# A GELU layer forward and backward: the first 256 rows of x turned by products on TensorE instead of by the DMA, the first q behind four units' pieces, and one transposed weight load in two

## The chip, the cores and the metric

One core of one Trainium2 chip runs the whole kernel in one launch. The metric is the device time of an execution in microseconds (us), the median of several. Engines are named as the profile names them: PE is TensorE (matmul; PEld is its weight load), DVE is VectorE, ACT is ScalarE, POOL is GpSimd, and SP is SyncE, which here only issues DMAs.

## The reference, cut to what matters

```python
B, S, D, F = 1, 2048, 448, 1792          # everything bf16
def forward(x, w1, b1, w2, b2):
    h = gelu(einsum("bsd,df->bsf", x, w1) + b1)      # tanh form of gelu
    return einsum("bsf,fd->bsd", h, w2) + b2
out, vjp = jax.vjp(forward, x, w1, b1, w2, b2)
return (out, *vjp(grad_out))             # out, gx, gw1, gb1, gw2, gb2
```

So three products come first for every block of rows: u = x·w1 (before the gelu), out = h·w2, and q = grad_out·w2ᵀ. Then gh = q·gelu'(u), and gx = gh·w1ᵀ. At the end come gw1 = xᵀ·gh and gw2 = hᵀ·grad_out, and the two bias sums.

## The kernel before, in words

**Stages.** The 2048 rows are four blocks of 512, taken in the order of `ROW0` (L54), so block 0 is rows 512 to 1023. F = 1792 is seven pairs of 128-column tiles, taken in the order `FP` = 1, 2, 3, 4, 5, 6, 0 (L56), so the first pair is columns 256 to 511. A step is one pair of one block, 28 in all. Both operands of u and q lie transposed in SBUF: `xT` and `gT` hold a block as 128 partitions by four slices of D (the fourth only half real, since 448 = 3·128 + 64), `w2T` holds w2 in the same way. All three come in by DMAs that transpose on the way, issued by SP in program order (L99 to L186). After the 28 steps (to about 177 us) come gw1 and gw2.

**What a step does.** PE makes u of the pair in two PSUM banks (three products of full depth 128 per tile, and one of depth 64, "the tail"). ACT copies u out with the bias (`copy_u`, L339; for the first two pairs DVE copies one of the two tiles), squares it (L354), makes gelu (L351, which writes `hT`) and a tanh (L363). DVE makes the slope of the gelu from these and at last multiplies it with q from PSUM (`dve_gh`, L401, which frees q's banks). Output units (`Unit`, L420: 128 rows of out or gx, in one bank) collect pieces, two products for each pair, as their `hT` or `ghT` comes.

**Products of half height.** Most products are issued as two of 64 rows each, one on the lower and one on the upper half of the array, side by side (`side_by_side`, L308; all have line 265, in `half_product`). A pair of them takes the array as long as one product of full height. Where one bank gets a product from the other half than before, `half_product` puts in a wait on the earlier one (L260 to L264). Products of full height are `pe_u_fulls` (L238, line 244), the tails with zeros (L502, line 505) and a unit's `emit` (L428, line 431).

**The start.** The order is written out by hand under `manual_schedule`. SP issues the transposing load of `xT[0]` in two halves of 256 rows (L146, L149), then a part of w1 (L154), w2 (L155), all of `gT[0]` (L156), `w2T` for columns 256 to 511 (L157), and so on. ACT issues w1 and its last 64 rows (`load_rest`) for columns 256 to 511 (L147, L148); behind its table load and a small activation (L151) it issues w1 for 512 to 767 (L152) and `load_rest` for 512 to 1023 (L153). POOL issues b1, which DVE turns into a column per tile (L192, L193) for `copy_u`. PE begins with `NWAKE` = 11 products on constant ones (L190), whose result nobody reads. Then it makes u of pairs 0, 1 and 2 (L507, L513, L519; pair 0 over the two halves of `xT[0]`), opens four units (L520 to L523), and L524 to L549 order what follows: pieces of units 0 and 1 for pair 0 at full height, pieces of units 2 and 3 side by side, the tails of u 2 and q 0, the rest of q 0 with units 2 and 3 between, and so on. The loop at L556 does the steps from 1.

Of the kernel before, what the change touches and what calls it, by code (L numbers as in the profile page):

```python
# [10 lines left out]
ALU = mybir.AluOpType  # L11
BF16 = mybir.dt.bfloat16
F32 = mybir.dt.float32
# [6 lines left out]
def kernel(  # L20
# [15 lines left out]
    nc = tc.nc  # L36
    P = 128
    B, S, D = x.shape
# [4 lines left out]
    KF = D // P  # L43
    DL = D - KF * P
    SB = 512
# [3 lines left out]
    NSTEP = NB * NPAIR  # L49
    NSINGLE = 12  # L50
    LEAD = 2
    NWAKE = 11
    STG = 5
    ROW0 = [SB, 2 * SB, 3 * SB, 0]  # L54
    WIDE = (0, 1)
# [3 lines left out]
    x2 = x.rearrange("b s d -> (b s) d")  # L59
# [4 lines left out]
    const = ctx.enter_context(tc.tile_pool(name="const", bufs=1))  # L64
# [14 lines left out]
    w2T = const.tile([P, KF + 1, F], BF16, name="w2T")  # L79
# [8 lines left out]
    def one_bank(n, name):  # L88
        return psum.tile([P, SB], F32, name=name, tag=f"one{n}")

    def two_banks(n, name):
        return psum.tile([P, 2, SB], F32, name=name, tag=f"two{n}")

    xT, gT = {}, {}

    def wide(src, r0, n, shift):
        return bass.AP(src.tensor, src.offset + r0 * D - shift, [[D, n], [1, (KF + 1) * P]])
# [11 lines left out]
    def load_g(b):  # L109
        t = blk.tile([P, KF + 1, SB], BF16, name="gT", tag="gT")  # L110
        r0 = ROW0[b]
        if b in WIDE:
            nc.sync.dma_start_transpose(out=t[:], in_=wide(g2, r0, SB, DL))
        else:
            nc.sync.dma_start_transpose(out=t[:, 1:KF + 1, :], in_=g2[r0:r0 + SB, DL:D])
            nc.sync.dma_start_transpose(out=t[:, 0, :], in_=g2[r0:r0 + SB, 0:P])
        gT[b] = t

    def load_w1(eng, f0, f1):
        return eng.dma_start(out=w1_f[:, :, f0:f1], in_=w1[0:KF * P, f0:f1].rearrange("(kt p) f -> p kt f", p=P))  # L120

    def load_rest(eng, f0, f1):
        return eng.dma_start(out=wt1[0:DL, f0:f1], in_=w1[KF * P:D, f0:f1])

    def behind(eng, transfer):
        tc.add_manual_dep(eng.nop().ins, transfer.ins.name, mybir.DependencyInfo(mybir.DependencyClass.Sync, mybir.DependencyReason.DATA),
                          reason="loads behind what is needed first")

    def load_w2(eng, t0, t1):
        return eng.dma_start(out=w2_sb[:, t0:t1, :], in_=w2[t0 * P:t1 * P, :].rearrange("(ft p) d -> p ft d", p=P))  # L130

    def load_w2T(f0, f1):
        if f0 > 0:
            nc.sync.dma_start_transpose(out=w2T[:, :, f0:f1], in_=wide(w2, f0, f1 - f0, DL))
        else:
            nc.sync.dma_start_transpose(out=w2T[:, :, 16:f1], in_=wide(w2, 16, f1 - 16, DL))
            nc.sync.dma_start_transpose(out=w2T[:, 1:KF + 1, 0:16], in_=w2[0:16, DL:D])

    AZ = tmp.tile([P, 12, SB], BF16, name="AZ", tag="AZ", bufs=1)
    ones = nc.const_aps.tensor(1.0, [P, SB], BF16)  # L140
    nc.vector.memset(wt1[DL:P, 256:768], 0.0)
    nc.gpsimd.memset(b1_rows[:], 0.0)
    nc.gpsimd.dma_start(out=b1_rows[0:NF, :], in_=b1.rearrange("(ft p) -> ft p", p=P))
    xT[0] = blk.tile([P, KF + 1, SB], BF16, name="xT", tag="xT")
    halves = [slice(0, SB // 2), slice(SB // 2, SB)]
    nc.sync.dma_start_transpose(out=xT[0][:, :, halves[0]], in_=wide(x2, ROW0[0], SB // 2, 0))  # L146
    load_w1(nc.scalar, 256, 512)  # L147
    load_rest(nc.scalar, 256, 512)  # L148
    nc.sync.dma_start_transpose(out=xT[0][:, :, halves[1]], in_=wide(x2, ROW0[0] + SB // 2, SB // 2, 0))  # L149
    warm = stg.tile([P, 1], F32, name="warm", tag="warm", bufs=1)  # L150
    behind(nc.scalar, nc.scalar.activation(out=warm[:], in_=ones[:, 0:1], func=ACT.Gelu_apprx_tanh))  # L151
    load_w1(nc.scalar, 512, 768)  # L152
    load_rest(nc.scalar, 512, 1024)  # L153
    load_w1(nc.sync, 768, 1024)  # L154
    load_w2(nc.sync, 2, 4)  # L155
    load_g(0)  # L156
    load_w2T(256, 512)  # L157
    load_w2(nc.sync, 4, 6)
    load_w1(nc.sync, 1024, 1280)
    load_rest(nc.sync, 1024, F)  # L160
# [27 lines left out]
    pw = two_banks(1, "pw")  # L188
    for w in range(NWAKE):
        nc.tensor.matmul(pw[:, 0, :], lhsT=ones[:, 0:P], rhs=ones, start=True, stop=True)  # L190
    for c in range(P // 32):
        nc.vector.transpose(b1_t16[c * 32:(c + 1) * 32, :], b1_rows[:, c * 32:(c + 1) * 32])  # L192
    nc.vector.tensor_copy(out=b1T[:], in_=b1_t16[:, 0:NF])  # L193
# [2 lines left out]
    PU, PQ = {}, {}  # L196
# [4 lines left out]
    def cols(p, a):  # L201
        return slice((2 * FP[p] + a) * P, (2 * FP[p] + a + 1) * P)
# [28 lines left out]
    def open_u(f):  # L231
        b, p = divmod(f, NPAIR)
        if p == 0:
            hT[b] = blk.tile([P, NF, SB], BF16, name="hT", tag="hT")
        banks = (2, 3) if f == 1 else (0, 1) if f < NSINGLE + LEAD else order_a[2 * (f % 2):2 * (f % 2) + 2]
        PU[f] = [one_bank(n, "pu") for n in banks]

    def pe_u_fulls(f):  # L238
        b, p = divmod(f, NPAIR)
        open_u(f)  # L240
        for rs in halves if f == 0 else [slice(0, SB)]:
            for a in range(2):
                for kt in range(KF):
                    nc.tensor.matmul(PU[f][a][:, rs], lhsT=w1_f[:, kt, cols(p, a)], rhs=xT[b][:, kt, rs],  # L244
                                     start=(kt == 0 and rs.start == 0), stop=False, skip_group_check=True)

    def half(up):
        return slice(DL, P) if up else slice(0, DL)

    def open_q(k):  # L250
        b, p = divmod(k, NPAIR)
        if p == 0:
            ghT[b] = blk.tile([P, NF, SB], BF16, name="ghT", tag="ghT")
        PQ[k] = two_banks(0 if k < NSINGLE else order_b[k % 2], "pq")

    LOW, HIGH = slice(0, DL), slice(DL, P)
    seen, count = {}, [0, 0]

    def half_product(bank, ps, w, m, hf, start, stop):
        if bank in seen and seen[bank][1] != hf.start and seen[bank][2] > count[1]:  # L260
            turn = nc.tensor.nop()
            tc.add_manual_dep(turn.ins, seen[bank][0], mybir.DependencyInfo(mybir.DependencyClass.Sync, mybir.DependencyReason.DATA),
                              reason="one bank from both row halves")
            count[1] = seen[bank][2]  # L264
        mm = nc.tensor.matmul(ps, lhsT=w, rhs=m, start=start, stop=stop, tile_position=(hf.start, 0), skip_group_check=True)  # L265
        count[0] += 1
        seen[bank] = (mm.ins.name, hf.start, count[0])

    def u_tail(f, a):
        b, p = divmod(f, NPAIR)  # L270
        hf = half(b not in WIDE)
        half_product(("u", f, a), PU[f][a][:], wt1[hf, cols(p, a)], xT[b][hf, KF, :], hf, False, True)
# [11 lines left out]
    def pe_tails(fs, ks):  # L284
        cross = bool(fs) and bool(ks) and (fs[0] // NPAIR in WIDE) != (ks[0] // NPAIR in WIDE)
        for k in ks:
            open_q(k)
        us = [(f, a) for f in fs for a in range(2)]
        qs = [(k, a) for k in ks for a in range(2)]
        if not us and len(ks) == 2:  # L290
            for a in range(2):
                q_tail(ks[0], a)
                q_tail(ks[1], a, swap=True)
            return
        for n in range(max(len(us), len(qs))):
            if n < len(us):
                u_tail(*us[n])
            if n < len(qs):
                q_tail(*qs[n], swap=cross)
# [8 lines left out]
    def side_by_side(one, other, part=slice(0, None)):  # L308
        for lo, hi in list(zip(one(LOW), other(HIGH)))[part]:
            half_product(*lo)  # L310
            half_product(*hi)
# [6 lines left out]
    def q_of(k, a, last=False):  # L318
        b, p = divmod(k, NPAIR)
        return lambda hf: [(("q", k, a), PQ[k][:, a, :], w2T[hf, kt, cols(p, a)], gT[b][hf, kt, :], hf, False, last and kt == KF)  # L320
                           for kt in range(1, KF + 1)]
# [6 lines left out]
    def units_side(uns, second, tiles=range(NF)):  # L328
        one, other = uns[::-1] if second else uns
        side_by_side(unit_of(one, tiles), unit_of(other, tiles))  # L330
        for un in uns:
            un.slots += len(tiles)
        if one.slots == 2 * NF:
            for un in uns:
                un.done = NPAIR
                open_units.remove(un)
                finished.append(un)
# [183 lines left out]
    for n in (2, 3):  # L521
        open_unit(one_bank(n, "ps")[:, 0:D])
    uns = [open_units[0:2], open_units[2:4]]  # L523
    for un in uns[0]:  # L524
        un.emit(0)

    g_swap = {}
    g_low = const.tile([P, SB], BF16, name="g_low")
# [12 lines left out]
    def tiles(p):  # L541
        return range(2 * p, 2 * p + 2)

    units_side(uns[1], False, tiles(0))
    pe_tails([2], [0])
    side_by_side(q_of(0, 0), q_of(0, 1))
    units_side(uns[1], True, tiles(0))
    side_by_side(q_of(0, 1, True), q_of(0, 0, True))
    units_side(uns[0], False, tiles(1))  # L549
    dve_chain("slope 0", "slope*h 0", "both 0", "cubic 1")  # L550
    copy_u(2, "aa")
# [94 lines left out]
    for n in range(nq):  # L646
# [25 lines left out]
        if nxt:  # L672
# [3 lines left out]
            uns = open_units[-2:]  # L676
# [5 lines left out]
        elif fs:  # L682
            uns, held = two_units(order_a[2:4]), two_units(order_a[0:2])
# [17 lines left out]
    for banks in (order_a[2:4], None, order_a[0:2], order_a[2:4]):  # L701
        if banks is None:
            open_two(0, 2)
            uns = open_units[-2:]
        else:
            uns = two_units(banks)
# [159 lines left out]
```

## Time and profile before

| | |
|---|---|
| time, median of 3 runs | 267.05 us (266.97 to 267.14) |
| time of the profiled execution | 267.09 us |
| its span (first to last instruction of the trace) | 265.3 us |
| PE busy | 261.6 us, 99% |
| DVE busy | 174.8 us, 66% |
| ACT busy | 137.4 us, 52% |
| POOL busy | 42.7 us, 16% |
| HBM read, written | 7.23 MB, 14.23 MB |

A row of the timeline gives the start, the time from there to the end, the engine, the line and the operands (written on the left of the arrow, read on the right), how many instructions were merged, and in brackets the idle time ahead of it with what ended it. Matmul records overlap: a product of 512 columns lasts 0.38 us in the record while the next one starts after 0.21 us. So the pace of PE is read from the distance of starts, and a busy share of 99% alone does not say that PE never waits.

### The profile page before, as it was taken

The page shows a single profiled execution, that of the slowest core. Times are in us where ns is not written, and L with a number is a line of the kernel's source. Part 1 is how long each engine was busy: PE and PEld are TensorE (multiplying, and loading weights), DVE is VectorE, ACT ScalarE, POOL GpSimd, SP SyncE. Part 2 cuts the span into 40 slices and gives each one's busy share as a digit, 9 for nine tenths or more (in the row PEclk, how much of TensorE's full clock was granted, in tenths as well). Part 3 has the DMA queues.
Part 4 walks back from the last instruction along what each step waited for, and adds up shares of the span by engine and source line. Part 5 has one row for each costly group of instructions (what it writes and reads, how often), then busy time and mean ns, then how long its engine had stood idle before and what let it go on. Part 6 is the DMA issues. An engine that isn't in the chain of part 4 may idle for free.

```text
span 265.3 us, 5207 instructions
## 1 busy us (share of the span) xinstructions
PE 261.6 (99%) x2171; PEld 148.9 (56%) x2171; DVE 174.8 (66%) x217; ACT 137.4 (52%) x164; POOL 42.7 (16%) x54
## 2 busy tenths in 40 slices
PE   8999999999999999999999999999999999999995
PEld 3444444444466565555658888864444765555554
DVE  1599999999998978769897731129999991000000
ACT  2799997887997686877749410022111111121111
POOL 1003003300302021010311111220700008900000
PEclk9999999999999999999999999999999999999999
DMA  7999999999999999465381359999211102999851
GB/s 177 234 239 197 215 216 153 227 101 259 282 220 193 248 206 268 89 171 110 95 161 49 67 125 308 349 164 276 81 40 40 49 22 56 212 216 224 203 129 35
DMA packets 111511, 44.47 MB, mean 168 GB/s; under 512 B 91104, under 2 KB 110272, under 8 KB 111488
## 3 DMA queue, kind: packets, MB, share of 16 engines
q1 hardware_dynamic: 104256, 35.79, 65.3%
q0 software_dynamic: 1984, 4.65, 7.2%
q10 hardware_dynamic: 5248, 3.71, 4.7%
q8 instruction: 17, 0.28, 0.4%
q14 instruction: 6, 0.05, 0.1%
HBM read 7.23 MB, written 14.23 MB: 81 GB/s over the span
## 4 chain that ended last, share of the span: by engine, by line
PE 99%; ACT 0%; issue 0%
PE ps L265 32%; PE ps_v L814 16%; PE pu L265 16%; PE pq L265 15%; PE ps_w L782 14%; PE ps_w L793 2%; PE pw L190 2%; PE pu L244 2%; PE pu L505 0%; PE ps L431 0%; ACT st L817 0%
## 5 line engine op out<-in xcount | busy, mean ns | idle before, releaser
L265 PE MATMUL pq<-gT,w2T 64*128 64x512 bf16 x386 | 55.6, 376 | 0.0
L265 PE MATMUL ps<-w_sb,hT 64*128 64x448 bf16 x440 | 49.0, 349 | 0.0
L265 PE MATMUL ps<-w1T_sb,ghT 64*128 64x448 bf16 x448 | 48.8, 349 | 0.0
L345 ACT ACTIVATE U<-pu,b1T 128x512 bf16<-128x512 f32 x54 | 33.5, 688 | 18.9 <-PE pu L265 14.4
L814 PE MATMUL ps_v<-g_nat,h_nat 128*128 128x448 bf16 (+1 forms) x240 | 42.6, 340 | 0.0
L403 DVE SCALAR_TENSOR_TENSOR ghT<-AZ,pq 128x1024 bf16<-128x1024 bf16 x28 | 33.9, 1218 | 12.3 <-PE pq L265 11.8
L265 PE MATMUL pu<-xT,w_f 64*128 64x512 bf16 x300 | 41.4, 376 | 0.0
L444 POOL DMA_DIRECT2D out_dram<-st x32 | 19.8, 625 | 133.3 <-DVE st L443 70.9
L265 PEld LDWEIGHTS <-ghT 64*128 64x128 bf16 x448 | 28.9, 94 | 15.3
L782 PE MATMUL ps_w<-gh_nat,x_nat 128*128 128x512 bf16 (+1 forms) x192 | 36.5, 352 | 0.0
L265 PEld LDWEIGHTS <-hT 64*128 64x128 bf16 x440 | 26.4, 94 | 17.0 <-issue 0.5
L265 PEld LDWEIGHTS <-w2T 64*128 64x128 bf16 x392 | 26.4, 94 | 14.9 <-PE pq L265 1.0
L814 PEld LDWEIGHTS <-h_nat 128*128 128x128 bf16 x240 | 23.3, 98 | 19.3 <-DMA out_dram<-st 0.3
L363 ACT ACTIVATE AZ<-AZ 128x1024 bf16<-128x1024 bf16 (+1 forms) x20 | 27.8, 1391 | 6.8 <-DVE AZ L359 6.8
L768 DVE TENSOR_TENSOR acc<-acc,gh_nat 128x1792 f32<-128x1792 f32 x14 | 30.0, 2142 | 0.5
L782 PEld LDWEIGHTS <-x_nat 128*128 128x128 bf16 x192 | 18.7, 98 | 17.9 <-issue 0.4
L354 ACT ACTIVATE AZ<-U 128x1024 bf16<-128x1024 bf16 (+1 forms) x21 | 28.2, 1342 | 0.9 <-DVE U L347 0.4
L351 ACT ACTIVATE hT<-U 128x1024 bf16<-128x1024 bf16 (+1 forms) x22 | 28.0, 1277 | 0.0
L817 ACT CAST st<-ps_v 128x448 bf16<-128x448 f32 (+1 forms) x15 | 7.6, 507 | 34.8 <-PE ps_v L814 34.8
L265 PEld LDWEIGHTS <-w_f 64*128 64x128 bf16 x300 | 16.2, 94 | 15.0 <-issue 0.7
L441 ACT CAST st<-ps 128x448 bf16<-128x448 f32 x16 | 7.8, 539 | 29.3 <-PE ps L265 27.6
L785 ACT CAST st<-ps_w 128x512 bf16<-128x512 f32 (+1 forms) x12 | 6.4, 532 | 27.7 <-PE ps_w L782 27.7
(58 smaller groups left out, 192.2 us busy)
## 6 DMA issues: line engine op xcount, KB each, us to landing
hT_dram<-hT SPq DMA_DIRECT2D x28, 256.0 KB, 3.2
out_dram<-st POOLq DMA_DIRECT2D x32, 112.0 KB, 4.7
x_nat<-in_x_dram SPq DMA_DIRECT2D x1, 1792.0 KB, 10.2
g_nat<-in_grad_out_dram SPq DMA_DIRECT2D x1, 1792.0 KB, 15.6
out_dram<-st ACTq DMA_DIRECT2D x13, 112.0 KB, 3.3
out_dram<-st ACTq DMA_DIRECT2D x9, 128.0 KB, 1.7
w_f<-in_w_dram SPq DMA_DIRECT2D x5, 192.0 KB, 3.8
w_sb<-in_w_dram SPq DMA_DIRECT2D x3, 224.0 KB, 3.8
```

What stands on the lines that cost most here:

```text
L265: mm = nc.tensor.matmul(ps, lhsT=w, rhs=m, start=start, stop=stop, tile_position=(hf.start, 0), skip_group_check=True)
L345: nc.scalar.activation(out=dst, in_=PU[f][a][:], func=ACT.Identity, bias=bias)
L351: nc.scalar.activation(out=rows(hT, r), in_=part_u(r), func=ACT.Gelu_apprx_tanh)
L354: nc.scalar.activation(out=part_a(ks), in_=part_u(ks), func=ACT.Square, scale=math.sqrt(3.0 * GELU_A * GELU_C))
L363: nc.scalar.activation(out=z, in_=z, func=ACT.Tanh, scale=-1.0 / 3.0)
L403: nc.vector.scalar_tensor_tensor(out=rows(ghT, [k]), in0=part_z([k]), scalar=1.0, in1=PQ[k][:], op0=ALU.subtract if single else ALU.add, o ...
L441: nc.scalar.copy(out=st[:, 0:D], in_=self.ps)
L444: pooled.append(nc.gpsimd.dma_start(out=(out2 if self.kind == "o" else gx2)[r:r + P, :], in_=st[:, 0:D]))
L768: last_sum[:] = [nc.vector.tensor_tensor(out=v, in0=in0, in1=gh_nat[:, b, :, j, :], op=ALU.add)]
L782: nc.tensor.matmul(ps[:, 0:n * P], lhsT=x_nat[:, st_, kt * P:(kt + 1) * P], rhs=gh_nat[:, b, ft0:ft0 + n, j, :], start=(st_ == 0), stop=(s ...
L814: nc.tensor.matmul(ps[:, 0:w], lhsT=h_nat[ft][:, st_, :], rhs=g_nat[:, st_, h * w:(h + 1) * w], start=(st_ == 0), stop=(st_ == NS - 1))
L817: done = nc.scalar.copy(out=o[:, 0:w], in_=ps[:, 0:w])
```

## The change

The load of `xT[0]`'s first half is no longer a transposing DMA. Its 256 rows come by a plain DMA into `x_rows`, which lies in a part of `AZ` that is not used until later (partition p gets rows 2p and 2p+1, 1792 bytes in one piece). DVE builds an identity matrix (`ident`): a row of column numbers by doubling, four 32x32 transposes for the row numbers, and a comparison. PE multiplies slices of `x_rows` with it, two products of 128 columns for each of the four slices of D, each writing every second column of a bank. ACT copies slices 0 and 2 out of PSUM, DVE slices 1 and 3. `NWAKE` goes from 11 to 7. The w1 load for columns 512 to 767 goes from ACT's queue to SP's. The first `w2T` load is cut into columns 256 to 383 and 384 to 511. In `pe_u_fulls` the two tiles alternate under each slice. All four units get their pieces for pair 0 at full height, and then q 0 is made by products of full height, with u 2's tails and q 0's tails at its end.

```diff
-    NWAKE = 11
+    NWAKE = 7
...
+    x_rows = AZ[:, 10:12, :].rearrange("p a s -> p (a s)")[:, 0:2 * D].rearrange("p (j d) -> p j d", j=2)
+    col = const.tile([P, P], F32, name="col")
+    row = const.tile([P, 32], F32, name="row")
+    ident = const.tile([P, P], BF16, name="ident")
+    nc.vector.memset(col[:, 0:1], 0.0)
+    for c in range(7):
+        nc.vector.tensor_scalar(out=col[:, 1 << c:2 << c], in0=col[:, 0:1 << c], scalar1=float(1 << c), scalar2=None, op0=ALU.add)
+    for c in range(P // 32):
+        nc.vector.transpose(row[c * 32:(c + 1) * 32, :], col[c * 32:(c + 1) * 32, c * 32:(c + 1) * 32])
+    nc.vector.tensor_scalar(out=ident[:], in0=col[:], scalar1=row[:, 0:1], scalar2=None, op0=ALU.is_equal)
     nc.vector.memset(wt1[DL:P, 256:768], 0.0)
...
-    nc.sync.dma_start_transpose(out=xT[0][:, :, halves[0]], in_=wide(x2, ROW0[0], SB // 2, 0))
+    nc.sync.dma_start(out=x_rows, in_=x2[ROW0[0]:ROW0[0] + SB // 2, :].rearrange("(p j) d -> p j d", j=2))
+    nc.vector.memset(xT[0][DL:P, KF, halves[0]], 0.0)
...
-    load_w1(nc.scalar, 512, 768)
     load_rest(nc.scalar, 512, 1024)
+    load_w1(nc.sync, 512, 768)
     load_w1(nc.sync, 768, 1024)
     load_w2(nc.sync, 2, 4)
     load_g(0)
-    load_w2T(256, 512)
+    load_w2T(256, 384)
+    load_w2T(384, 512)
...
+    xb = [one_bank(2, "xb"), one_bank(3, "xb"), two_banks(0, "xb")[:, 0, :], two_banks(1, "xb")[:, 1, :]]
+    for kt in range(KF + 1):
+        m = P if kt < KF else DL
+        for j in range(2):
+            nc.tensor.matmul(xb[kt][0:m, halves[0]][:, j::2], lhsT=x_rows[:, j, kt * P:kt * P + m], rhs=ident[:], start=(j == 0),
+                             stop=(j == 1), skip_group_check=True)
+        if kt % 2:
+            nc.vector.tensor_copy(out=xT[0][0:m, kt, halves[0]], in_=xb[kt][0:m, halves[0]])
+        else:
+            nc.scalar.copy(out=xT[0][0:m, kt, halves[0]], in_=xb[kt][0:m, halves[0]])
...
-            for a in range(2):
-                for kt in range(KF):
+            for kt in range(KF):
+                for a in range(2):
...
-    for un in uns[0]:
+    for un in uns[0] + uns[1]:
         un.emit(0)
+    open_q(0)
+    for a in range(2):
+        for kt in range(1, KF + 1):
+            nc.tensor.matmul(PQ[0][:, a, :], lhsT=w2T[:, kt, cols(0, a)], rhs=gT[0][:, kt, :], start=(kt == 1), stop=False,
+                             skip_group_check=True)
...
-    units_side(uns[1], False, tiles(0))
-    pe_tails([2], [0])
-    side_by_side(q_of(0, 0), q_of(0, 1))
-    units_side(uns[1], True, tiles(0))
-    side_by_side(q_of(0, 1, True), q_of(0, 0, True))
+    for a in range(2):
+        u_tail(2, a)
+        half_product(("q", 0, a), PQ[0][:, a, :], w2T[HIGH, 0, cols(0, a)], gT[0][HIGH, 0, :], HIGH, False, True)
     units_side(uns[0], False, tiles(1))
```

## The prediction, made before the result was known

> **What bounds the kernel now.** I read the chain of waits first. It is PE for 99% of the span, so time is won only where PE starts sooner, runs faster, or waits less. The change touches the first 15 us, so I took PE's timeline there, in small windows, for the distance of starts.
>
> ```profile
> 0.77 4.85 PE pw L190 x11
> 5.62 1.87 PE pu L244 x12
> 7.92 1.29 PE pu L244 x6
> 9.65 1.29 PE pu L244 x6
> 10.95 0.85 PE ps L431 x4
> ```
>
> This is the chain's beginning (start, length): 11 products on ones, and then u of pairs 0, 1, 2 and the units, with nothing between. Real work starts with the first record of L244, at 5.41. It could not start much sooner, as the next view (DMA issues around 0.73, last column us from issue to landing) shows:
>
> ```profile
> w_f<-in_w_dram ACTq DMA_DIRECT2D x1, 192.0 KB, 2.7
> xT<-in_x_dram SPq DMA_TRANSPOSE x1, 4.6
> ```
>
> Both were issued at 0.73. The weights were there at 3.43, the turned x only at 5.33. So the first thing that PE waits for is the turned half of x; the wake products merely fill that time.
>
> ```profile
> 4.56 0.15 PEld L190 LDWEIGHTS <-const-bfloat16-1.0 128*128 128x128 bf16 x1 [0.28 <-issue]
> ...
> 4.99 0.63 PE L190 MATMUL pw<-const-bfloat16-1.0 128*128 128x512 bf16 x1
> ...
> 6.27 0.57 PE L244 MATMUL pu<-xT,w_f 128*128 128x256 bf16 x2
> 6.48 0.58 PE L244 MATMUL pu<-xT,w_f 128*128 128x256 bf16 x3
> 6.67 0.60 PE L244 MATMUL pu<-xT,w_f 128*128 128x256 bf16 x4
> 6.78 0.49 PE L244 MATMUL pu<-xT,w_f 128*128 128x256 bf16 x3
> ```
>
> These are starts from narrow windows. Products on ones start 0.43 us apart for 512 columns, those of L244 0.21 us apart for 256 columns up to 6.48, then 0.19, and from 6.67 on 0.11. So PE runs at half pace from 0.77 to about 6.65 and at full pace after (later, 512 columns go every 0.215 us). The page's row of granted clock shows 9 in the first slices too; it does not show this step, the starts do. **So an early start is worth half:** what PE begins before 6.65 advances at half pace.
>
> From 7.75 on ACT has the chain. Its timeline is copy u 0, square, gelu, copy u 1, tanh, square, gelu, copy u 2 without a break but the 0.4 us in which it waits for DVE's copy:
>
> ```profile
> 7.75 0.69 ACT L345 ACTIVATE U<-pu,b1T 128x512 bf16<-128x512 f32 x1 [4.44 <-PE pu L505]
> 8.81 1.06 ACT L354 ACTIVATE AZ<-U 128x1024 bf16<-128x1024 bf16 x1 [0.38 <-DVE U L347]
> ...
> 14.13 1.25 ACT L345 ACTIVATE U<-pu,b1T 128x512 bf16<-128x512 f32 x2
> ```
>
> PE waits for it twice: L431 starts 0.30 after the last product of u 2 where 0.215 is due (gelu ends at 10.81), and u 3 at 15.05 goes on only at 15.43, when copy u 2 (14.13 + 1.25) has freed its second bank. That is 0.085 + 0.165 = 0.25 us of PE waits. After 15.43 PE's starts are 0.19 to 0.22 apart, which is its full pace, and the shares of the chain name nothing else. So the end of the kernel follows the moment at which u 0 is finished, through ACT, up to 15.43, and PE itself from there.
>
> **The change, part by part.**
>
> *The new first load.* x_rows is 224 KB, issued at 0.73 as before. Its row is not in the trace. The nearest is w1's first load, 192 KB issued in the same moment: 2.7 us. Upper bound: the small w1 tail issued right behind it took 4.0 us. So it lands between 3.43 and 4.73; I take 3.6, near the row of its own kind and size. The seven wake products end their slots at 0.77 + 7 · 0.427 = 3.71 (the eighth of before started there). So the first turning product goes at about 3.75.
>
> *The identity.* DVE starts at 0.85: one tiny memset, seven additions (nearest row: the 128x14 cast, 0.17), four 32x32 transposes (0.20 each on b1), and a 128x128 comparison (0.13 to 0.3). 0.05 + 1.2 + 0.8 + 0.25 = 2.3, so it is ready at 3.2, 0.5 before it is needed. The two memsets behind it (0.27 and less) end before the first copy. If every small operation took 0.27, it would be 4.4, and the start 0.65 later.
>
> *The turning.* Eight products of 128 columns. A half-pace product streams 256 columns in 0.213, so 128 in 0.107; its weight load takes 0.152 (row above). Bounds for the distance: 0.107 if loads hide, 0.26 if nothing overlaps. I take 0.152, since every product needs a new load and, in the rows of L190, a load starts with the product before it. So 8 · 0.152 = 1.2 us, and PE is free at 4.95 (4.6 to 5.85). Beside it, ACT copies slice 0: its two products end near 4.25 (a 256-column half-pace record lasts 0.42, so 128 columns some 0.32), the nearest copy (128x256 from PSUM to bf16 on ACT) took 0.37, so slice 0 is there at 4.65. Slice 1 (DVE, 512 columns took 0.75, so 0.4 to 0.5 here) is there at about 5.1 and is needed 0.43 after slice 0. Slices 2 and 3 have more time. ACT's queue ahead of its copies holds only the DMA issue of load_rest (3.34 to about 3.85), since the w1 issue has left it. So the copies hide behind the turning; without that cover they would cost 0.4.
>
> *Real work starts at 4.95 instead of 5.41*, and the gain is half of that: (5.41 − 4.95) / 2 = **0.23 us**. Bounds: 4.65 gives 0.38; 5.85 gives −0.22. The second half of xT is needed 1.28 later, at 6.2. Its DMA is issued at about 1.25 instead of 2.13 (a plain issue takes 0.46 to 0.58, not 1.35) and needs 3.7 to 4.6, so it lands by 5.85.
>
> *SP's queue.* It loses 0.8 us of issue in front and gains the w1 issue (0.42 to 0.58) and one more issue for w2T. So w1 for 512 to 767 goes at 2.5 instead of 3.34 on ACT and lands near 6.6 (before 7.44, needed at 7.5). gT goes at 4.0 to 4.1 instead of 4.61 and lands by 10.3. w2T's first part, issued near 7.8, lands at 11.3, the second, by the before row of the pair, at 12. All behind it keeps its place or moves up; before, each had 0.8 us or more (w2 4 to 5: 13.48 against 14.28; w1 1024 to 1279: 14.00 against 15.05; w2T 512 to 767: 15.62 against 16.95). b1 lands at 4.79; its transposes now stand behind DVE's two copies and end near 6.5, needed at 7.5.
>
> *The order of units and q.* The same array time: four side-by-side pairs (0.19 each) become four full products, six pairs of q (0.215) six full ones, and the tails stay. q 0 begins 1.5 us behind hT instead of 1.2, and u 2's tails go from 12.12 to about 13.5 and end near 13.9, when ACT comes to copy u 2 (14.13 − 0.23). Cover just enough; if not, 0.1 to 0.2 lost. What it removes is a gap of 0.09 at 11.45 and 0.02 at 12.36; both lie beside ACT's chain, so they give nothing. q 0 is complete at 14.0, as before, and gh 0 (15.56) does not notice.
>
> **Sum:** −0.23 on the profiled execution, 267.09 → 266.86; it lies 0.04 over the median of 267.05, so 266.82. I say **266.8** (−0.1%).
>
> **The rivals.**
>
> *The step to full pace comes later (slower).* The wake and the real work ran without a gap before. Now half-filled turning (0.107 of each 0.152), a wait for x_rows, or for slice 0, lies at 3.7 to 5. If that makes PE's count start again at 4.95, the same 5.88 us (0.77 to 6.65) end at 10.83, not 6.65: 4.18 us more at half pace, 2.09 lost, less 0.23 won and 0.25 in which PE waits for ACT: +1.6, 268.65. It decides as soon as the step falls more than about 0.5 us later. For it: nothing in the trace says how much idleness the step allows. Against: there is little real idleness, and much of it is covered. [...] Chance 0.20.
>
> *The rows come late or the turning is slow.* x_rows at 4.3 or a distance of 0.26 puts the start to 5.6 or 5.85: 267.1 to 267.3. Chance 0.13.
>
> *The new order also takes PE's waits away.* If ACT's chain is looser than I read it, 0.25 + 0.11 go with the 0.23: 266.5. Against: copies and gelu stand back to back. Chance 0.12.
>
> **The numbers.** Forecast 0.55 (266.65 to 267.05), the rivals 0.20, 0.13, 0.12. A measurement of this kernel can tell about 0.2% (0.53 us) from no change. Faster by that: most of the third rival and a tail of the forecast, 0.17. Slower: the late step and a little of the second, 0.22. Within: 0.61. The range 266.1 to 267.6 holds all but the late step.
>
> **What would show it.** The first L244 record near 4.95 and its copies before it; the distance of 256-column starts falling to 0.11 at 6.65 again; ACT's first copy of u near 7.5; then every later record of PE 0.2 to 0.3 us earlier, to the end. Wrong if the step has moved, if the turning products start more than 0.2 us apart, or if PE waits for w2T near 12.

## The result, and the profile after

The changed kernel takes **268.18 us** (median of 16 runs, 267.20 to 269.09) against 266.89 for the kernel before (16 runs of the same time on the chip, 266.40 to 268.20). The ratio is 1.0044 with a 95% interval of 1.0030 to 1.0059: slower by 0.44%, about 1.2 us, and above the predicted range (266.1 to 267.6). (The ratios in this document are not those of the medians, which lie 1.29 us apart here.) The profiled execution took 269.09 us, its span is 267.0 us; it is the longest of the 16, so a second profile of the same kernel (`e16_changed_again`, 268.18 us, span 266.1) is used beside it.

The chain of waits, in order of time (start, us, what), now begins otherwise. Before, it was PE from 0.77 on. After:

```profile
1.19 1.58 SPq L160
...
4.70 3.40 SPq L113
8.14 1.27 SPq L134
9.45 1.26 SPq L134
...
41.52 5.67 DMA w1T_sb<-in_w_dram
```

SPq is SP's queue of DMA issues. From 0.73 to 41.52 the chain is one issue of SP behind the other, 0.04 to 0.06 us apart. Then it is the transfer of w1T's tiles 12 and 13, for which PE stood still; PE has the chain from 47.23 on. (These two tiles are called "the last of w1T" below; one more load behind it, of tiles 0 and 1, is needed later.) In before SP was just as busy, but in that profile PE waits for none of its loads.

The start, as PE's timeline of the changed kernel in narrow windows shows it (a row's start is that of its first record):

```profile
4.26 0.93 PE L207 MATMUL xb<-ident,AZ 128*128 128x128 bf16 x3
4.69 0.85 PE L207 MATMUL xb<-ident,AZ 128*128 128x128 bf16 x2
5.12 0.62 PE L207 MATMUL xb<-ident,AZ 128*64 128x128 bf16 x2
5.25 0.49 PE L207 MATMUL xb<-ident,AZ 128*64 128x128 bf16 x1
5.67 0.28 PE L266 MATMUL pu<-xT,w_f 128*128 128x256 bf16 x1
```

Products of 128 columns start 0.21 us apart (4.26, 4.47, 4.69), not 0.152, and the two changes between weights of 128 and of 64 columns (4.69 to 5.12, 5.25 to 5.67) take 0.43 each. The turning took 3.71 to 5.67. All the same u 0 was finished sooner: its first tail starts at 6.99, 7.33 before, because from 5.79 on products of 256 columns already start 0.11 apart, which in before began at 6.67. ACT follows. The row that was at 7.75, in ACT's timeline:

```profile
7.41 0.69 ACT L367 ACTIVATE U<-pu,b1T 128x512 bf16<-128x512 f32 x1 [1.81 <-PE pu L527]
```

So 0.34 us were won, a little more than forecast. They are still there (0.23) at 24 us. Then PE's timeline of the changed kernel has two rows of a kind that before had nowhere (in brackets the idle time ahead and its releaser):

```profile
24.30 0.56 PE L287 MATMUL ps<-w_sb,hT 64*128 64x448 bf16 x4 [0.57 <-DMA w_sb<-in_w_dram]
...
47.23 0.56 PE L287 MATMUL ps<-w1T_sb,ghT 64*128 64x448 bf16 x4 [0.69 <-DMA w1T_sb<-in_w_dram]
```

The same instructions started at 23.80 and 45.56 in before, without a wait:

```profile
23.80 0.54 PE L265 MATMUL ps<-w_sb,hT 64*128 64x448 bf16 x4
...
45.56 0.54 PE L265 MATMUL ps<-w1T_sb,ghT 64*128 64x448 bf16 x4
```

Beside the first of the two there is, after the change, a wait of 0.57 for w1's columns from 1536 on (`w_f`). With them the lead of 0.23 becomes a lag of 0.82 after 24 us and of 1.67 after 47, and 1.67 is what the span has more (267.0 against 265.3). A part of the time lies outside the span: device time less span is 2.14 us here (median of the runs, 2.08 to 2.18) and 1.77 in before.

The loads came late because SP came late. SP's timeline of before at two places, and then of the changed kernel (start, length of the issue):

```profile
8.33 1.30 SPq L134 DMA_TRANSPOSE w2T<-in_w_dram  x1
9.68 0.58 SPq L130 DMA_DIRECT2D w_sb<-in_w_dram  x1
...
34.90 3.18 SPq L113 DMA_TRANSPOSE gT<-in_grad_out_dram  x1
38.12 2.63 SPq L180 DMA_TRANSPOSE w1T_sb<-in_w_dram  x2
```

```profile
8.14 2.58 SPq L134 DMA_TRANSPOSE w2T<-in_w_dram  x2
10.76 0.58 SPq L130 DMA_DIRECT2D w_sb<-in_w_dram  x1
...
38.18 3.29 SPq L113 DMA_TRANSPOSE gT<-in_grad_out_dram  x1
41.52 2.71 SPq L192 DMA_TRANSPOSE w1T_sb<-in_w_dram  x2
```

The first part of w2T, one issue of 1.30 before, is now two that take 1.27 and 1.26: half the columns cost the queue as much as all. SP was 0.2 ahead at that point and is 1.1 behind after it, 2.1 at 23 us and 3.4 at 41.5; the last of w1T landed at 47.22 instead of 41.82.

### The profile page after: what moved, and what is told of

Read it like the earlier page. It is cut to its first block, busy times and chain, and to the rows that moved or that the text cites. A ratio compares the mean times of both kernels' runs of the same rounds, so it can differ in the third digit from the quotient of the medians.

```text
span 267.0 us, 5214 instructions
## 1 busy us (share of the span) xinstructions
PE 261.8 (98%) x2164; PEld 151.5 (57%) x2165; DVE 178.2 (67%) x233; ACT 138.3 (52%) x166; POOL 42.9 (16%) x54
## 4 chain that ended last, share of the span: by engine, by line
PE 81%; SPq 15%; DMA 2%; issue 1%; ACT 0%
PE ps L287 27%; PE ps_v L839 16%; PE ps_w L807 14%; PE pq L287 11%; PE pu L287 11%; SPq L134 4%; SPq L113 3%; PE ps_w L818 2%; DMA w1T_sb<-in_w_dram 2%; SPq L192 2%; SPq L120 1%; SPq L103 1%; SPq L130 1%; SPq L160 1%; SPq L136 1%
## 5 line engine op out<-in xcount | busy, mean ns | idle before, releaser
L287 PE MATMUL pq<-gT,w2T 64*128 64x512 bf16 x374 | 54.3, 376 | 0.0
L287 PE MATMUL ps<-w_sb,hT 64*128 64x448 bf16 x432 | 47.9, 349 | 0.6 <-DMA w_sb<-in_w_dram 0.6
L287 PE MATMUL pu<-xT,w_f 64*128 64x512 bf16 x300 | 41.5, 376 | 0.2
L287 PEld LDWEIGHTS <-ghT 64*128 64x128 bf16 x448 | 29.8, 94 | 15.3 <-issue 1.0
L287 PEld LDWEIGHTS <-w_f 64*128 64x128 bf16 x300 | 16.8, 94 | 14.8 <-issue 0.7
```

## The experiments

Two theories fit this profile. **Theory S**: a transposing load has a fixed price on SP's queue, the second part of w2T adds it, and loads that had a margin before come late. **The rival, R**: the new start or the new order on PE sets other DMAs against each other, and the second w2T issue is harmless. A third question was the 0.37 us outside the span. Each ratio is to the kernel before, run beside it on the same chip, with its 95% interval.

### The second w2T load alone

`e1_changed_one_load` is the changed kernel with one w2T load; `e2_before_two_loads` is the kernel before with two; `e3_before_spare_load` is the kernel before with a load of 16 rows that nobody reads.

```diff
 # e1, on the changed kernel
-    load_w2T(256, 384)
-    load_w2T(384, 512)
+    load_w2T(256, 512)
 # e2, on the kernel before
-    load_w2T(256, 512)
+    load_w2T(256, 384)
+    load_w2T(384, 512)
 # e3, on the kernel before
     load_w2T(256, 512)
+    spare = const.tile([P, 16], BF16, name="spare")
+    nc.sync.dma_start_transpose(out=spare[:], in_=w2[0:16, 0:P])
```

> The changed kernel with the first w2T load in one piece again. Theory S (SP's queue): each transposing load costs SP about 1.26 us of issue whatever its size, so the second piece puts every later load some 1.1 us later; in one piece the loads behind it are issued 1.2 to 1.3 us sooner (w2 rows 512 to 767 at about 9.5 instead of 10.76), the three waits of TensorE for DMAs (0.57 and 0.57 near 24, 0.69 near 47) go, and the time is 266.3 to 266.9. Rival R (the turning and the new order of q cost it, or the w1 load that SP now issues): the waits stay and the time is 267.6 to 268.2.

> The kernel before with only the first w2T load cut in two. Theory S: SP's later issues come 1.2 to 1.3 us later, TensorE begins to wait for w2 and w1 near 23 to 25 and for w1T near 46, and the time is 0.4 to 1.5 us over before (267.3 to 268.4). Rival R: no change, 266.7 to 267.1.

> The kernel before with one more transposing load of 16 rows (4 KB, into a spare tile that nobody reads) behind the first w2T load. Theory S says that SP's issue counts and not the bytes: the issue takes 1.2 us and the time is as in the kernel before with w2T in two (267.3 to 268.4). If the bytes or the transposed rows counted, one sixteenth of a 256-row load would cost 0.1 us at most, and the time would be that of before (266.7 to 267.1). Rival R: no change either.

Measured: e1 268.16 us, ratio 1.0026 (1.0008 to 1.0044); e2 267.71, 1.0034 (1.0012 to 1.0055); e3 267.81, 1.0024 (1.0010 to 1.0039). The profiled run of e2 took 273.67 us, 6 us more than its median, and no view of it is used. SP's timeline of e3:

```profile
8.50 1.30 SPq L134 DMA_TRANSPOSE w2T<-in_w_dram  x1
9.84 1.22 SPq L159 DMA_TRANSPOSE spare<-in_w_dram  x1
11.11 0.58 SPq L130 DMA_DIRECT2D w_sb<-in_w_dram  x1
```

Sixteen rows take the queue as long as 256 (1.22 against 1.30), and the kernel before becomes slower with nothing else touched. PE's timeline of e3 at 45 to 47 us has the wait of the changed kernel, and one for the next block of grad_out:

```profile
45.73 0.39 PE L267 MATMUL pq<-gT,w2T 64*128 64x512 bf16 x1 [0.31 <-DMA gT<-in_grad_out_dram]
...
46.51 0.56 PE L267 MATMUL ps<-w1T_sb,ghT 64*128 64x448 bf16 x4 [0.18 <-DMA w1T_sb<-in_w_dram]
```

What follows: S holds for e2 and e3, that one more issue costs 0.6 to 0.9 us here, and it is the issue and not the bytes. But e1 should have come back to 266.3 to 266.9 and did not: 268.16 is what the rival gave (267.6 to 268.2). Its median is level with the changed kernel's (268.18); its ratio is 0.18% lower, with intervals that overlap. So taking the second load out of the changed kernel is not shown to win back what adding it to before cost. In e1's profile the waits near 24 us are gone, as S says, and the lead of 0.46 lasts to 43 us; then gT of the next block (landed 45.59, before 40.50) and the last of w1T (46.43) come late all the same. S alone is not all.

### Cheaper queues

`e4_changed_w1_on_act` puts the w1 load for columns 512 to 767 back on ACT's queue. `e5` to `e7` leave out the two loads of 16 rows that SP issues later (L137 and L167 in before): 16 rows of w2 are then zeros in q, so a part of the result is not computed. e5 does it to the kernel before, e6 to e1, e7 to the changed kernel. `e8_old_order` is e1 with the order of units and q of before: only the turning with its identity and seven wake products, the w1 move and the alternating tiles are left of the change.

```diff
 # e4, on the changed kernel
+    load_w1(nc.scalar, 512, 768)
     load_rest(nc.scalar, 512, 1024)
-    load_w1(nc.sync, 512, 768)
 # e5, e6, e7
-            nc.sync.dma_start_transpose(out=w2T[:, 1:KF + 1, 0:16], in_=w2[0:16, DL:D])
...
-    nc.sync.dma_start_transpose(out=w2_first[:], in_=w2[0:16, 0:P])
...
-    nc.gpsimd.tensor_copy(out=w2T[DL:P, 0, 0:16], in_=w2_first[0:DL, :])
+    nc.gpsimd.memset(w2T[:, :, 0:16], 0.0)
```

> The changed kernel with the w1 load for columns 512 to 767 back on ACT's queue (w2T still in two). Theory S: SP is rid of one plain issue of 0.5 us, so its later loads come 0.5 us sooner, the waits of TensorE shrink from 1.9 to about 0.9 us in all, and the time is 267.3 to 267.8. If the plain load did not matter, it stays at 268.2. Rival R in its form that this load alone is to blame: 266.5 to 266.9.

> The kernel before without its two transposing loads of 16 rows (w2_first and the last piece of w2T; the first 16 columns of w2T are zeros instead, so q is computed without these 16 rows of w2). Theory S: SP has 2.4 us less to issue before gT[1] and the rest of w1T, so these land 2 to 4 us sooner and TensorE never waits for them; the runs of before at 268 and over go, and what is left is TensorE's own time: 266.4 to 267.0, no run over 267.6. Rival R (the loads are not near the bound in the kernel before): the same spread as before.

> The changed kernel with w2T's first load in one piece and without the two transposing loads of 16 rows (zeros in their place). Theory S: with SP relieved by 1.3 and 2.4 us no load is late, the 0.3 to 0.5 us won at the start reach the end, and the time is 266.0 to 266.7, below before. Rival R (the turning or the order costs something later on TensorE, ScalarE or VectorE): 267.2 or more, with no wait for a DMA in the trace.

> The changed kernel (w2T in two) without the two transposing loads of 16 rows (zeros in their place). Theory S: the waits near 24 us for w2 and w1 (1.05 us in the profile of the changed kernel) stay, since these loads stand ahead of the two; the wait for w1T near 47 goes. So the time lies between: 266.9 to 267.6. Rival R: as the changed kernel, 268.0 to 268.3.

> The changed kernel with w2T in one load and with the old order of the units and q 0 (so the kernel before with the turning, 7 wake products and the w1 load on SP). Theory S: the order moves no load, so the time is that of the changed kernel with one load, 267.6 to 268.2, with waits for gT[1] and w1T. Rival O (the new order of q 0 costs): 266.5 to 267.0. Against the new order: if q 0 now waits for w2T near 12 us, 0.2 to 0.4 us more than with the new order.

Measured: e4 269.44, 1.0090 (1.0073 to 1.0107); e5 267.00, 1.0006 (0.9995 to 1.0017); e6 267.72, 1.0039 (1.0013 to 1.0065); e7 267.47, 1.0027 (1.0013 to 1.0041); e8 267.33, 1.0012 (1.0000 to 1.0024).

e4 was a miss, the slowest of this group. On ACT the two loads came behind the small activation: w1 for 512 to 767 was issued at 3.34 and landed at 8.54, `load_rest` was issued only at 4.72 and landed at 11.62. The products that need them were due sooner: PE's weight loads waited 1.5 us for the first and 2.1 for the second. The lead of 0.35 became a lag of 2.6 by 17 us.

e5 was to bring gT of the next block and w1T in 2 to 4 us sooner. The time is that of before, and the loads did not come sooner. SP's timeline of e5, where before has 34.90 and 38.12:

```profile
34.95 3.31 SPq L112 DMA_TRANSPOSE gT<-in_grad_out_dram  x1
38.30 2.64 SPq L177 DMA_TRANSPOSE w1T_sb<-in_w_dram  x2
```

Two issues of 1.2 us are gone, and others took longer instead: the w2T load for columns 1024 to 1279 took 3.32 (2.71 in before), the first two of w1T together 5.96 (4.54). The last of w1T landed at 42.60 (41.82). So issues added early on delayed what follows (e2, e3), but issues taken away further on won nothing back: from about 17 us on, a sum of fixed issue times does not give the pace of this queue.

e7 lies in the range that S gave (266.9 to 267.6), but not for its reason. S had the waits near 24 us stay and the one for w1T go; the profile has none near 24, and still waits 0.8 us for w1T, which landed at 46.95. e6 was to be the fastest (266.0 to 266.7) and came out where its rival stood (267.2 or more). Its profiled run, at 267.14, has no wait worth naming (w1T at 45.20) and a span of 265.0, but its runs reach from 266.76 to 270.53. It differs from e7 by the second w2T load alone and is no faster (1.0039 against 1.0027, the intervals overlap).

S also missed for e8, which was to take 267.6 to 268.2 with waits for gT and w1T. It is 0.3 us slower than before by the median, and its spans are not (median 265.2, profiled 264.8): what it loses lies outside the span. Its profile shows what becomes of a better start: ACT leads by 1.00 us at 10 us and by 0.46 at 29; in between, PE, which comes sooner, waits for w2T near 12 and for w1 near 16.

### What is outside the span, and what the order does

`e9_before_identity` is the kernel before with the identity built by DVE and not used. `e10_order_alone` is the kernel before with the new order of units and q. `e11_pool_identity` and `e12_pool_full_width` are e8 with the identity built by POOL (12 also turns all four slices at a width of 128 columns). `e13_before_padding` adds twenty one-column memsets on DVE to the kernel before. `e14_old_order_230` is e8 with three of DVE's small memsets moved to POOL; `e15_full_width_230` is e14 with all slices 128 wide.

```diff
 # e11, on e8
-    nc.vector.memset(col[:, 0:1], 0.0)
...
-    nc.vector.tensor_scalar(out=ident[:], in0=col[:], scalar1=row[:, 0:1], scalar2=None, op0=ALU.is_equal)
+    make_identity(nc, ident[:])
 # e13, on the kernel before
+    pad = const.tile([P, 32], F32, name="pad")
+    for c in range(20):
+        nc.vector.memset(pad[:, c:c + 1], 0.0)
 # e14, on e8 (and so for wt1 and xT[0])
-    nc.vector.memset(col[:, 0:1], 0.0)
+    nc.gpsimd.memset(col[:, 0:1], 0.0)
 # e15, on e14
-        m = P if kt < KF else DL
+        m = P
```

> The kernel before with VectorE's identity built at its start and not used (13 more VectorE instructions, done by 3.5 us, while VectorE waits for b1 anyway). In the runs so far the time less the span was 1.72 to 1.85 us without the turning and 2.08 to 2.23 with it. Theory I (these VectorE instructions make the execution longer outside the span): time less span 2.1 to 2.2, span unchanged at about 265.3, so 0.3 to 0.4 us over before. Rival: time less span stays 1.77 and the time is that of before; then another part of the turning (its DMA, products or copies) lengthens it.

> The kernel before with only the new order of the units and of q 0 (full-height q behind all four units' pieces). Theory S: no load moves, so the span stays within 0.3 us of before (265.0 to 265.6) and time less span is 1.77. Rival O (the order costs later): the span is 0.5 us or more over before, with waits for gT[1] or w1T.

> The kernel of the old order with the turning, one w2T load and w1 on SP, but the identity made by GpSimd (a memset and an affine_select) instead of VectorE. Theory I: time less span falls from 2.15 to about 1.77, and the time is 266.6 to 267.0, 0.3 below the same kernel with VectorE's identity. Rival: time less span stays near 2.15.

> As the run with GpSimd's identity, with the fourth slice turned by products of 128 output rows instead of 64 (its upper 64 rows meet zero rows of w1). In the traces so far TensorE starts the two 64-row products 0.24 (full pace) to 0.43 us (half pace) after the product before and the next 128-row one again so much later, where 0.11 and 0.21 are due. If that is the switch between widths, the two gaps go, u 0 starts 0.25 to 0.45 us sooner where the second half of x is there, and the span is 0 to 0.3 us shorter. Rival (the gaps are waits for something else): they stay.

> The kernel before with 20 tiny VectorE memsets of a spare tile at its start, done while VectorE waits for b1 anyway. Time less span was 1.77 with 217 or 230 VectorE instructions in the trace (before; before with the identity) and 2.14 with 233 (all runs of the turning with VectorE's identity). Theory N (the number of VectorE instructions, past some bound between 230 and 233, lengthens the execution outside the span): 237 instructions give 2.1 to 2.2, with the span unchanged, so 0.35 us over before. Rival: 1.77, and it is something else in the turning.

> The kernel of the run with the old order (turning, one w2T load, w1 on SP) with three of its VectorE memsets on GpSimd, so that VectorE has 230 instructions again. Theory N: time less span 1.77 instead of 2.15, span as in that run (264.6 to 266.3, median 265.2), so 266.7 to 267.1 at the median and 0.35 below it. Rival: 2.15 stays.

> As the run before it, with the fourth slice turned by products of 128 output rows. With GpSimd's identity the two gaps at the switch of width were to be seen against the run without; here, where TensorE starts at 3.7, they are worth 0.2 to 0.5 us of TensorE's start, as long as the second half of x is there (it landed at 5.7 to 6.2 and was waited for in some runs). Span 0 to 0.3 us below the run before it, 266.4 to 267.0. Rival: x's second half hides it, no difference.

Measured: e9 266.95, 0.9996 (0.9986 to 1.0006); e10 267.21, 1.0007 (0.9997 to 1.0016); e11 274.68 and e12 274.48, 1.028 both; e13 267.14, 1.0012 (0.9999 to 1.0025); e14 267.05, 1.0009 (0.9991 to 1.0026); e15 267.07, 1.0014 (0.9997 to 1.0032).

The time outside the span goes by the number of DVE's instructions. The page's busy line (engine, us, share, count) of before, e13, e14 and e8, each from its own kernel:

```profile
PE 261.6 (99%) x2171; PEld 148.9 (56%) x2171; DVE 174.8 (66%) x217; ACT 137.4 (52%) x164; POOL 42.7 (16%) x54
```

```profile
PE 261.5 (99%) x2171; PEld 148.2 (56%) x2171; DVE 175.4 (66%) x237; ACT 137.4 (52%) x164; POOL 42.5 (16%) x54
```

```profile
PE 261.5 (99%) x2175; PEld 148.8 (56%) x2175; DVE 178.0 (67%) x230; ACT 138.1 (52%) x166; POOL 43.3 (16%) x57
```

```profile
PE 260.8 (98%) x2175; PEld 148.3 (56%) x2175; DVE 178.1 (67%) x233; ACT 138.3 (52%) x166; POOL 42.6 (16%) x54
```

With 217 (before, e2, e3, e5, e10), 220 (e11, e12) or 230 instructions (e9, e14, e15) on DVE, time less span is 1.75 to 1.79 us (medians of the runs); with 233 (changed kernel, e1, e4, e6 to e8, e16) or 237 (e13) it is 2.06 to 2.16. Twenty idle memsets on the kernel before make it (e13: its span is 265.1, no longer than before's), the 13 instructions of the identity alone do not (e9, against its theory), and moving three memsets to POOL unmakes it (e14 against e8: 1.77 against 2.15). The instructions of all engines together do not order it: the profile has 5227 in e13 and 5236 in e14. In device time the step is less sure: the interval of e13 includes 1, and its median is only 0.11 us over before, since its median span is 0.2 shorter. What the chip does in that time no view shows.

e10 says that the order by itself is not measurably slower. Its profiled run has a lag of 0.6 us from late w1 columns, its median span is 265.4.

e11 and e12 were misses, and show two other things. POOL's timeline of e11 and PE's:

```profile
1.95 0.22 POOL masks.py:197 MEMSET ident<- 128x128 bf16 x1
9.70 0.28 POOL masks.py:199 TENSOR_SCALAR_AFFINE_SELECT ident<-ident 128x128 bf16<-128x128 bf16 x1 [7.53 <-issue]
```

```profile
10.04 2.00 PE L199 MATMUL xb<-ident,AZ 128*128 128x128 bf16 x8 [6.13 <-POOL ident masks.py:199]
```

POOL's second step started 7.5 us after its first with nothing to wait for that the trace shows, and PE, which stood for 6.13 us, ran the turning at half pace (2.00 us for the eight products), as it had run its last wake products before the wait.

e14 and e15 tell the two halves of the turning's time apart. PE's timeline from the fifth turning product on, of e14 and then of e15:

```profile
4.61 1.28 PE L206 MATMUL xb<-ident,AZ 128*128 128x128 bf16 x4
5.82 0.41 PE L265 MATMUL pu<-xT,w_f 128*128 128x256 bf16 x2
```

```profile
4.54 1.14 PE L207 MATMUL xb<-ident,AZ 128*128 128x128 bf16 x4
5.39 0.79 PE L266 MATMUL pu<-xT,w_f 128*128 128x256 bf16 x3
```

With 64-column weights in the last slice 1.21 us pass to the first real product, with 128 columns throughout 0.85: the changes of width cost 0.36. Neither version is faster than the kernel before beyond what the measurement can tell; no version here beats it.

### The changed kernel once more

`e16_changed_again` has no edit: it is the changed kernel, profiled a second time.

> The changed kernel itself once more, for a second profile. Theory S: TensorE again waits for loads of SP's queue (w2 and w1 near 24 us, or gT[1] and w1T near 46), 0.5 to 2 us in all, whatever the moment of its clock's step; time 267.5 to 268.5. Rival: no such waits in this profile, while the time is still 1 us over before.

Measured: 268.38 us, 1.0055 (1.0034 to 1.0075), span of the profiled run 266.1, as S said for this run. The waits for DMAs in it behind the start, of PE and of its weight loads:

```profile
PE ps L287 <- DMA w1T_sb<-in_w_dram: 0.7, 1, 0.7
```

```profile
PEld L287 <- DMA w_f<-in_w_dram: 0.3, 1, 0.3
PEld L551 <- DMA w2T<-in_w_dram: 0.3, 1, 0.3
```

These are the late loads again: w2T's second part near 12, w1 near 24, w1T at 46.3 instead of 45.56. A run at the median has them too, smaller.

### All profiled runs side by side

"Lead" is how much sooner than in before ACT starts a given gelu; minus means later. The span of every run shown is 265.3 less its lead at 53 us, within 0.1. "Outside" is the median of device time less span. e2, e11 and e12 are not in the table.

| kernel | last of w1T lands | lead at 10 us | lead at 53 us | span | outside |
|---|---|---|---|---|---|
| before | 41.82 | 0 | 0 | 265.3 | 1.77 |
| e13 | 41.81 | 0.14 | 0.14 | 265.1 | 2.06 |
| e14 | 42.39 | 0.17 | 0.16 | 265.1 | 1.77 |
| e5 | 42.60 | 0.35 | 0.23 | 265.1 | 1.76 |
| e9 | 43.32 | −0.01 | −0.19 | 265.5 | 1.79 |
| e10 | 44.57 | 0.09 | −0.53 | 265.8 | 1.79 |
| e8 | 44.97 | 1.00 | 0.46 | 264.8 | 2.15 |
| e4 | 45.15 | 0.35 | −2.60 | 267.9 | 2.15 |
| e6 | 45.20 | 0.51 | 0.30 | 265.0 | 2.15 |
| e15 | 45.39 | 0.32 | 0.18 | 265.1 | 1.77 |
| e16 | 46.27 | 0.25 | −0.75 | 266.1 | 2.11 |
| e1 | 46.43 | 0.56 | −0.89 | 266.2 | 2.13 |
| e3 | 46.51 | 0.09 | −0.95 | 266.3 | 1.76 |
| e7 | 46.95 | 0.19 | −1.47 | 266.8 | 2.16 |
| changed | 47.22 | 0.34 | −1.67 | 267.0 | 2.14 |

Where the last of w1T lands by 45.4, at most 0.14 us is lost at 46 us; where it lands at 46.3 or later, 0.5 to 1.1 us are. (The lags of e4, e9 and e10 come from earlier loads.)

## Why the prediction was wrong

**The step that failed is the one on SP's queue, "All behind it keeps its place or moves up".** It let the second w2T load in as "one more issue" and gave it no duration. The runs put it at 1.26 us, as long as the whole load, and the trace of before already had the rows that say so: loads of 16 rows at L167 and L137 with issues of 1.18 and 1.22. The terms beside it were too small as well. gT was to go at 4.0 to 4.1 and went at 4.70, since the second half of xT took 1.58 to issue (1.28 in before), the w1 issues for 512 to 1023 took 1.09, and the w2 issue behind them 0.69 (0.47). So only 0.2 us of slack was left at the first w2T load (8.14 against 8.33) to pay 1.26 from, and w2 4 to 5, w1 1024 to 1279 and w2T 512 to 767 landed 0.28, 0.39 and 0.79 later than before, not sooner.

**The check of margins stopped too early.** The prediction compared landing and need up to 16.95 us, found 0.8 us or more, and went no further. The loads that hurt lie behind: w2 8 to 13 had 1.5 us in before (landed 22.29, needed 23.80) and the last of w1T 3.7 (41.82, 45.56). SP issues without a break from 0.73 to past 47 us, and in the changed kernel the delay was not made up on the way but grew, from 1.1 us at 10.8 to 3.4 at 41.5 and 5.4 in the landing. Why it grew is not shown; e5 says that fewer issues need not undo it.

**The time outside the span had no term.** The sum went from one span to another with the difference of before. It is 0.37 us larger, about a third of the loss of 1.2 us.

**The gain was there.** x_rows landed at 3.63 (forecast 3.6), the identity was ready at 3.45 (3.2), the copies took 0.37 on ACT and 0.42 on DVE as forecast. The turning was too cheap by 0.76: 1.96 us, not 1.2, from 0.21 a product instead of 0.152 and two changes of width. That alone would have made the rival "the turning is slow" true. It was made good by the step to full pace, which "6.65 again" had fixed: it came between 5.25 and 5.79 here. Together they gave 0.34 where 0.23 was forecast: two wrong terms cancelled, which is luck. Of this, 0.1 was lost again by 17 us (in e1, e6, e7 and e16 too): copy u 2 came at 13.87 where 13.80 was due, behind the tails of u 2. That is the item "cover just enough". The three signs by which the prediction was to be known wrong all came: the step had moved, the turning products started 0.21 apart, and PE's weight load waited 0.2 us for w2T near 12.

**The step to full pace moved where PE's first products did not.** It came at 6.65 in before and at 6.2 in e13, before 3.9 in e3 and e10, and these four begin with the same products on PE; it came before 3.9 in e8 too, and between 5.2 and 6.0 in the changed kernel and e14. The moments lie at least 2.7 us apart, so a single profile of the start can't size a gain there. What sets the moment is not shown.

**The rival of the late step gave 268.65, close to the result, and is false all the same.** That a pause makes PE take its 5.88 us at half pace again was an assumption. In no profiled run but e11 and e12, with 6 us of waiting, was PE at half pace after 6.7 us, and the turning's own gaps did not put the step later (by 5.79 in the changed kernel, 6.65 in before); in e3 PE waited 1.2 us just after it and went on at full pace. After the 6.13 us of e11 it was at half pace, but it had been at half pace before them too, so no run here shows PE falling back. The third rival, that PE's waits for ACT would go too, did not come: the lead was 0.34 at 10 us and 0.23 at 24, not more.

**The account.** Of the 1.2 us, 0.37 lies outside the span and about 0.8 in it. That the part in the span is PE waiting for late loads is shown by the two profiles of the changed kernel, whose lags of 1.67 and 0.75 at 53 us arise at these waits. That the second w2T load can cost as much is shown on the kernel before (0.6 to 0.9 us in e2 and e3). That it is what costs it in the changed kernel is argued only: without it the ratio is still 1.0026 (e1), of which 0.37 us (0.14%) is the time outside, and in e1's profile gT and w1T come late without it.

**What stays open.** The same program order on SP brought the last of w1T in at 42.39 (e14) and 45.39 (e15), with issues from 22.5 us on that differ in length (the one for L136 took 1.46 and 2.90). What lengthens them no run here settles; it decides in which runs PE waits, and so the wide spread of the changed kernel's times. A rival that was not tested is the transfers themselves: in before, the profile puts the busy share of the DMA engines at 0.79 to 1.27 in every 4 us from 8 to 48, so an issue may have had to wait for them. Whether the new order has a share in it when x is turned is open as well: e1 and e8 differ by it, 1.0026 against 1.0012, and their intervals overlap.

## What to carry to other kernels

Count the issues on a queue, and not only the bytes: a load split in two took twice the issuing time here (1.27 and 1.26 us against 1.30), and a load of 16 rows added to a queue that runs without a break made the kernel slower (1.0024, e3), with PE's waits 36 us behind the place of the edit (0.31 and 0.18 us, at 45.73 and 46.51). So check the margin of each later load to the end of that queue's work, landing against first use, before calling an extra issue free. Do not count on the reverse: taking issues off the same queue gave no time back (1.0006, e5). And read a gain at the start from several profiles, since the moment of TensorE's step to full pace moved by at least 2.7 us between kernels that start alike (6.65 in before, before 3.9 in e3 and e10), and compare device time with the span, since what is added can lie outside every view (0.37 us here).

## What the runs showed of the hardware that was not expected

- At the same place of the queue, 8 to 10 us after the start, a transposing load of 16 rows held SP for 1.22 us (e3), one of 128 for 1.27 (changed kernel) and one of 256 for 1.30 (before); the plain ones behind it took 0.47 to 0.58. Further on, a load of 256 rows took up to 3.37 (changed kernel), and one of 512 rows took 3.67 already at 4.61 (before). So by these rows a transposing issue took more than twice as long as a plain one.
- A change between weights of 128 and of 64 columns on TensorE took 0.43 us from start to start at half pace (0.21 without the change; changed kernel) and 0.24 at full pace (0.11).
- Device time less span rose from 1.77 to 2.15 us between 230 and 233 instructions on VectorE (e14, e8).
- The first affine select of GpSimd began 7.5 us after the memset before it (e11); seven additions, four transposes and a comparison made the same identity on VectorE in 2.65 us (0.80 to 3.45, changed kernel).
